# k'v of linear attention as two 64-column products per pair of heads, the pairs two at a time

## The chip, the cores and the metric

The kernel runs on one core of a Trainium2 chip. Its time is the device time of one execution in microseconds (us), as the median of several runs. A profiled execution gives the trace: for each engine (PE is TensorE's matmuls, PEld its loads of weights, DVE VectorE, ACT ScalarE, POOL GpSimd, SP the queue that issues DMAs) when each instruction began and how long it took.

## What is computed

Three layers follow each other: linear attention with a normalised output, a feed-forward layer with h cos(h) between its two matrices, and a soft mixture of experts.

```python
batch, n_heads, seq, head_dim = (8, 8, 576, 64)
kv = np.einsum('bhsd,bhse->bhde', k, v)
out = np.einsum('bhsd,bhde->bhse', q, kv)
rms = np.sqrt(np.mean(out * out, axis=-1, keepdims=True) + 1e-06)
x = (out / rms * g_norm)          # then laid out as 4608 tokens x 512
h = x @ w_in                      # 512 x 2048
g = h * np.cos(h)
x = g @ w_out                     # 2048 x 512
logits = x @ phi                  # 32 slots, softmax over tokens (d) and over slots (c)
slot_input = d.T @ x
...                               # two layers per expert on the slots
return c @ slot_out
```

The change is in the first line alone: kv, one 64 x 64 matrix for each batch and head.

## The kernel before

The 4608 tokens go through in 12 blocks of 384 (index j), and each block in 16 steps (index f) over 128 of the 2048 columns of w_in. Three blocks cover two batches (384 tokens of the one, 384 of the other, 192 of each). All is float32; h is computed in three float32r products.

In each step TensorE runs `main`, 12 matmuls of 384 columns into one of three buffers named h. The cosine chain then takes ScalarE (fr, tt), VectorE (tt), ScalarE (the sine, L401) and VectorE (gT, which frees the buffer, and the transpose tr). Between two mains stands side work that tables in PLAN place by step; a step number of 16 or more means the next block. The order on every engine is written out by these tables, and each engine follows its own queue.

The side work, by the names of its tiles: `kvps` is k'v, `ops` the attention output of 128 tokens, `xTps` their transposes, `l` the logits of four steps (four matmuls, each into 32 partitions), `lr` their sum over the four partition groups, `ldT` a transpose of the exponentials, `ab` the sum over slots, `tr` and `wps` transposes and products with w_out in the first two blocks, `eo` a product of the experts in the tail.

k'v of a batch is four calls of `kv_pair`, one for each pair of heads. A pair multiplies 128 columns of k (two heads) with 128 columns of v, over four chunks of 128 rows and one remainder of 64 (`kz`, `vr`), into 128 x 128 of PSUM. Of this only the two 64 x 64 blocks on the diagonal are wanted; two copies (L140) take them to `kvbd`, which holds the other blocks at zero.

From batch 4 on, the four pairs of a batch stand in steps 14, 17, 18 and 19 of a block. Logits stand in steps 6, 10, 14 and 18, lr in step 19. Batches 2 and 3 have a table of their own, `K`; batch 1's pairs all stand in the first step, and batch 0's ahead of it. Banks for kvps, ops, xTps, lr and others come from one pool of four, `at_bank`, in the order of the requests.

Of the kernel before, what the change touches and what calls it, by code (L numbers as in the profile page):

```python
# [40 lines left out]
    stop=None,  # L41
    start=(
# [4 lines left out]
    ),  # L47
# [17 lines left out]
    xs=(1, 1, 1),  # L65
    xT=(7, 11, 14),
    lo=(1, 0, 0),
    kv=(14, 17, 18, 19),
    rg=(11, 18),
    kvl=0,  # L70
    ql=13,
# [4 lines left out]
def tile_linear_attention__ffn_cos__soft_moe(  # L76
# [14 lines left out]
    nc = tc.nc  # L91
# [44 lines left out]
    def at_bank(name):  # L136
        return ps_a.tile([128, 512], F32, tag="at", name=name)

    def copy_on(e, out, in_):
        (nc.vector.tensor_copy if e else nc.scalar.copy)(out=out, in_=in_)  # L140


    q_t, kv_t, vr_t = {}, {}, {}
    kz = rem_p.tile([128, 2, 512], F32, tag="kr", name="kz")
# [31 lines left out]


    def kv_pair(b, pr):
        ps = at_bank("kvps")[:, 0:128]
        t = kv_t.pop((b, pr))  # L180
        for r in range(4):
            nc.tensor.matmul(out=ps, lhsT=t[:, 0, r, :], rhs=t[:, 1, r, :], start=(r == 0), stop=False)  # L182
        cc = slice(pr * 128, pr * 128 + 128)
        nc.tensor.matmul(out=ps, lhsT=kz[:, b % 2, cc], rhs=vr_t[b // 2][:, cc], start=False, stop=True)  # L184
        t = kvbd[b % 2]
        e = PLAN["ke"][b] if b < 2 else 2
        copy_on(e, t[0:64, pr, 0:64], ps[0:64, 0:64])
        copy_on(e, t[64:128, pr, 64:128], ps[64:128, 64:128])

        kv_done.add((b, pr))  # L190

# [642 lines left out]
    for b in range(1, B):  # L834
        p, i = divmod(b, 2)
        n, sl = 3 * p - 2 + i, PLAN["kv"]
        if b < 4:
            n, sl = PLAN["K"][b - 1]
        for pr in range(4):
            at2(n, sl[pr], kv_pair, b, pr)  # L840
# [96 lines left out]
    def token(t, f):  # L937
        k, *arg = t.split(".")
        if k.upper() in steps:
            out = int(k.islower())  # L940
            w = int(arg[0]) if arg else f + (PLAN["LO"] if out else PLAN["LI"])
            if w < NF and (arg or w >= (PLAN["PO"] if out else PLAN["PI"])):
                ck(k.upper(), w, out)
                steps[k.upper()](w, out)
        elif arg:
            a = int(arg[0])
            dict(kv=lambda: kv_pair(0, a), ao=lambda: att_out(0, a), xs=lambda: att_xs(0, a),
                 xT=lambda: att_xT(0, a), lo=lambda: att_lo(0, a), warm=lambda: warm(a),
                 win=lambda: load_win(a), wout=lambda: load_wout(a), lkv=lambda: load_kv(a // 4, a % 4),
                 rem=lambda: load_rem(a) if a == 0 else load_kz(0, 1), q=lambda: load_q(a))[k]()  # L950
        else:
            j = int(k[1])
            f -= L * j
            if 0 <= f < NF:
                dict(m=main, s=lambda j, f: run(side, j, f), f=fr_tt, r=round_off, p=lambda j, f: run(post, j, f),
                     b=cos_b, c=cos_c, e=lambda j, f: run(fin, j, f), l=lambda j, f: run(loads, j, f))[k[0]](j, f)
# [103 lines left out]
```

## Time and profile before

| what | value |
|---|---|
| three runs | 719.67, 717.18, 719.83 us; median 719.67 |
| profiled execution | 720.89 us |
| its span, first to last instruction | 719.0 us |
| TensorE busy | 689.0 us, 96% |
| VectorE busy | 527.1 us, 73% |
| ScalarE busy | 443.8 us, 62% |
| kvps, matmul passes of L182 and L184 | 256 and 64 |

The first three lines are times of the whole execution; the others are from the trace, where busy time is the union of an engine's instructions. A float32 matmul stands in the trace as two passes, each a load of weights (PEld) and a matmul (PE): 32 pairs of four matmuls at L182 make 256. Passes overlap, so one pass's own duration (280 ns in the mean for kvps) is longer than the distance to the next; prices are read from start to start.

### The profile page before, as it was taken

To read this page: it belongs to the slowest core of one execution; us is meant where nothing else is said; L and a number is where in the kernel's file an instruction comes from. 1 tells how busy PE (TensorE), PEld (TensorE's weight loads), DVE (VectorE), ACT (ScalarE), POOL (GpSimd) and SP (SyncE) were. 2 spreads that over 40 slices of the span, in tenths; PEclk is the share of its full clock that TensorE was granted. 3 is DMA by queue.
4 is the path that set the end of the run, shared out by engine and by line. 5 is a ranking of instruction groups with operands and counts; after the bars stand their busy time and mean duration, and the time that the engine had idled before them with its cause. 6 is when DMAs were issued, how large, how long until landed. Compare 5 with 4: busy or idle time off the path is not lost.

```text
span 719.0 us, 13016 instructions
## 1 busy us (share of the span) xinstructions
PE 689.0 (96%) x4780; PEld 574.3 (80%) x4780; DVE 527.1 (73%) x1101; ACT 443.8 (62%) x929; POOL 106.5 (15%) x104
## 2 busy tenths in 40 slices
PE   7879999999999999999999999999999999999984
PEld 7768998886998987998898879889979797864353
DVE  2998998477888878788888887888887874345144
ACT  2567997675666676575576756656757557551143
POOL 2342333100302111112012011110120210000400
PEclk9998999999999999999999999999999999999997
DMA  9953452022742674564525745735249278989997
GB/s 323 377 190 138 176 188 78 4 80 100 210 122 67 183 206 124 169 179 103 147 77 148 205 146 154 213 84 152 73 117 305 51 242 269 348 321 347 356 370 320
DMA packets 73886, 134.09 MB, mean 186 GB/s; under 512 B 8416, under 2 KB 50016, under 8 KB 73056
## 3 DMA queue, kind: packets, MB, share of 16 engines
q1 hardware_dynamic: 73824, 133.27, 58.7%
q8 instruction: 38, 0.62, 0.3%
q14 instruction: 24, 0.20, 0.1%
HBM read 91.29 MB, written 13.63 MB: 146 GB/s over the span
## 4 chain that ended last, share of the span: by engine, by line
PE 82%; DVE 9%; ACT 4%; issue 2%; DMA 1%; SPq 0%; POOL 0%; DVEq 0%; ACTq 0%
PE h L375 50%; PE ab L533 5%; PE kvps L182 4%; PE l L458 4%; PE ops L201 4%; PE xTps L233 2%; PE tr L431 2%; PE eo L689 2%; PE eh L663 2%; DVE gT L410 1%; DVE tt L396 1%; PE l L467 1%; PE fo L714 1%; PE kvps L184 1%; DVE tr L416 1%
## 5 line engine op out<-in xcount | busy, mean ns | idle before, releaser
L375 PE MATMUL h<-xt,w 128*128 128x384 f32 x2304 | 438.0, 342 | 1.6 <-DVE xt L246 1.2
L375 PEld LDWEIGHTS h<-xt,w 128*128 128x128 f32 x2304 | 397.2, 189 | 29.1 <-DVE gT L410 8.9
L401 ACT ACTIVATE fr<-tt 128x384 f32<-128x384 f32 x192 | 100.4, 524 | 136.5 <-DVE tt L396 136.0
L410 DVE TENSOR_TENSOR gT<-fr,h 128x384 f32<-128x384 f32 x186 | 102.8, 553 | 58.6 <-ACT fr L401 58.4
L213 POOL TENSOR_TENSOR ri<-ss,mhalf 128x8 f32<-128x8 f32 x36 | 65.5, 1825 | 430.8 <-DVE ss L211 430.8
L396 DVE SCALAR_TENSOR_TENSOR tt<-tt,fr 128x384 f32<-128x384 f32 x192 | 106.5, 559 | 28.9 <-ACT tt L391 27.5
L391 ACT ACTIVATE tt<-fr 128x384 f32<-128x384 f32 x192 | 100.9, 525 | 6.1
L389 ACT ACTIVATE fr<-h 128x384 f32<-128x384 f32 x192 | 92.7, 483 | 18.2 <-PE h L375 18.0
L416 DVE STREAM_TRANSPOSE tr<-gT 128x384 f32<-128x384 f32 x144 | 83.3, 579 | 5.1 <-DVE gT L410 0.2
L237 ACT ACTIVATE xt<-xTps,gn 128x512 fp32r<-128x512 f32 x36 | 24.6, 686 | 27.8 <-PE xTps L233 27.4
L182 PEld LDWEIGHTS kvps<-kv 128*128 128x128 f32 x256 | 31.8, 191 | 9.9 <-issue 6.4
L201 PE MATMUL ops<-kvA,q 128*64 128x128 f32 (+1 forms) x384 | 38.2, 278 | 1.3 <-ACT g L140 1.3
L201 PEld LDWEIGHTS ops<-kvA,q 128*64 128x64 f32 (+1 forms) x384 | 33.9, 164 | 5.2 <-issue 2.8
L182 PE MATMUL kvps<-kv 128*128 128x128 f32 x256 | 35.2, 280 | 1.8 <-DMA kv<-in_kv 1.7
L246 DVE SCALAR_TENSOR_TENSOR xt<-xTps,gn,xt 128x512 fp32r<-128x512 f32 x36 | 26.4, 738 | 12.8 <-ACT xt L237 12.5
L313 POOL TENSOR_TENSOR w<-st_m,w 128x512 fp32r<-128x512 f32 x16 | 26.7, 1670 | 54.3 <-ACT w L308 41.1
L533 PE MATMUL ab<-g,d 128*32 128x512 f32 x288 | 33.5, 596 | 0.3 <-DVE d L522 0.3
L458 PE MATMUL l<-gT,wp 128*32 128x384 f32 x312 | 33.3, 498 | 0.0
L140 ACT COPY g<-tr 128x384 f32<-128x384 f32 (+1 forms) x64 | 23.4, 393 | 7.7 <-PE tr L431 7.4
L210 DVE TENSOR_REDUCE ss<-sq 128x8 f32<-128x512 f32 x33 | 22.2, 672 | 5.0 <-ACT sq L208 4.8
L208 ACT ACTIVATE sq<-ops 128x512 f32<-128x512 f32 x33 | 19.6, 593 | 9.1 <-PE ops L201 9.1
L222 DVE TENSOR_TENSOR xs<-ops,ri 128x512 f32<-128x512 f32 x33 | 22.3, 682 | 2.4 <-POOL ri L213 2.4
(133 smaller groups left out, 631.3 us busy)
## 6 DMA issues: line engine op xcount, KB each, us to landing
g<-tr SPq DMA_DIRECT2D x288, 96.0 KB
kv<-in_kv SPq DMA_DIRECT2D x32, 512.0 KB
ew<-in_w SPq DMA_DIRECT2D x26, 512.0 KB
ew<-in_w SPq DMA_DIRECT2D x43, 256.0 KB
out<-ot SPq DMA_DIRECT2D x12, 768.0 KB
q<-in_qT SPq DMA_DIRECT2D x11, 768.0 KB
rw<-in_w_in SPq DMA_DIRECT2D x16, 512.0 KB
st_b<-in_w_outT SPq DMA_DIRECT2D x16, 512.0 KB
```

The lines of the kernel that those rows point to most:

```text
L182: nc.tensor.matmul(out=ps, lhsT=t[:, 0, r, :], rhs=t[:, 1, r, :], start=(r == 0), stop=False)
L201: nc.tensor.matmul(out=ps[p0:p0 + n, pr * 128:(pr + 1) * 128], lhsT=q_t[j][:, pr, c0:c0 + n], rhs=kvbd[b % 2][:, pr, :], start=True, stop= ...
L213: nc.gpsimd.tensor_tensor(out=ri[:, :, 0], in0=ss, in1=mhalf, op=ALU.pow)
L375: nc.tensor.matmul(out=ps, lhsT=w[:, a, kk, :], rhs=x[:, b, kk, :], start=(n == 0), stop=(n == 3 * KD - 1))
L389: nc.scalar.activation(out=fr, in_=ps, func=AF.Copy, bias=0.25, scale=INV_2PI)
L391: nc.scalar.activation(out=tt, in_=fr, func=AF.Copy, bias=ROUND_M)
L396: nc.vector.scalar_tensor_tensor(out=tt, in0=tt, scalar=-ROUND_M, in1=fr, op0=ALU.add, op1=ALU.subtract)
L401: nc.scalar.activation(out=fr, in_=tt, func=AF.Sin, scale=-TWO_PI_DOWN)
L410: nc.vector.tensor_tensor(out=g, in0=fr, in1=h_t.pop((j, f)), op=ALU.mult)
L416: nc.vector.transpose(out=tr_t[j, h][:, :, o, :], in_=g.rearrange("p (b t) -> p b t", t=32))
L458: nc.tensor.matmul(out=l_t[j][32 * o:32 * o + 32, :], lhsT=wp[:, f, :], rhs=gT_t.pop((j, f)), start=(c == 0), stop=(c == (2 if j == NB - 1 ...
L533: nc.tensor.matmul(out=ps[32 * c:32 * c + 32, :], lhsT=d[:, t, :], rhs=gs[c // 2][t][:, (c % 2) * 512:(c % 2) * 512 + 512], start=(t == 0) ...
```

## The change

`kv_pair` no longer forms the full 128 x 128 product. For each chunk it issues two matmuls, one per head: 64 columns of k and 64 of v into partitions 0 to 63 or 64 to 127 of the bank, both in columns 0 to 63. The second copy reads its block at the new place. In the table, the second pair of a batch moves from step 17 to step 14 and the fourth from step 19 to step 18, from batch 4 on.

```diff
-    kv=(14, 17, 18, 19),
+    kv=(14, 14, 18, 18),
...
     def kv_pair(b, pr):
-        ps = at_bank("kvps")[:, 0:128]
+        ps = at_bank("kvps")[:, 0:64]
         t = kv_t.pop((b, pr))
+        hh = [slice(0, 64), slice(64, 128)]
         for r in range(4):
-            nc.tensor.matmul(out=ps, lhsT=t[:, 0, r, :], rhs=t[:, 1, r, :], start=(r == 0), stop=False)
-        cc = slice(pr * 128, pr * 128 + 128)
-        nc.tensor.matmul(out=ps, lhsT=kz[:, b % 2, cc], rhs=vr_t[b // 2][:, cc], start=False, stop=True)
+            for h in hh:
+                nc.tensor.matmul(out=ps[h], lhsT=t[:, 0, r, h], rhs=t[:, 1, r, h], start=(r == 0), stop=False)
+        for h in hh:
+            cc = slice(pr * 128 + h.start, pr * 128 + h.stop)
+            nc.tensor.matmul(out=ps[h], lhsT=kz[:, b % 2, cc], rhs=vr_t[b // 2][:, cc], start=False, stop=True)
         t = kvbd[b % 2]
         e = PLAN["ke"][b] if b < 2 else 2
         copy_on(e, t[0:64, pr, 0:64], ps[0:64, 0:64])
-        copy_on(e, t[64:128, pr, 64:128], ps[64:128, 64:128])
+        copy_on(e, t[64:128, pr, 64:128], ps[64:128, 0:64])
```

On TensorE, in a block that holds the pairs of batch 4, from the logits of step 14 to the main of step 20, before:

```order
L458 MATMUL l<-gT,wp 32x384 x4
L182 MATMUL kvps<-kv 128x128 x4
L184 MATMUL kvps<-vr,kz 128x128
L233 MATMUL xTps<-ident,xs 128x128 x4
L375 MATMUL h<-xt,w 128x384 x36
L182 MATMUL kvps<-kv 128x128 x4
L184 MATMUL kvps<-vr,kz 128x128
L375 MATMUL h<-xt,w 128x384 x12
L458 MATMUL l<-gT,wp 32x384 x4
L182 MATMUL kvps<-kv 128x128 x4
L184 MATMUL kvps<-vr,kz 128x128
L375 MATMUL h<-xt,w 128x384 x12
```

and of the change, the same place (its lines stand three further down):

```order
L461 MATMUL l<-gT,wp 32x384 x4
L184 MATMUL kvps<-kv 64x64 x8
L187 MATMUL kvps<-vr,kz 64x64 x2
L184 MATMUL kvps<-kv 64x64 x8
L187 MATMUL kvps<-vr,kz 64x64 x2
L236 MATMUL xTps<-ident,xs 128x128 x4
L378 MATMUL h<-xt,w 128x384 x48
L461 MATMUL l<-gT,wp 32x384 x4
L184 MATMUL kvps<-kv 64x64 x8
L187 MATMUL kvps<-vr,kz 64x64 x2
L184 MATMUL kvps<-kv 64x64 x8
L187 MATMUL kvps<-vr,kz 64x64 x2
```

Each group of logits now has two pairs behind it, and between the two groups four mains (48 matmuls) follow each other without other work; lr in step 19 has no pair behind it any more.

On VectorE, the same block in step 14 and the steps behind it, before:

```order
L416 STREAM_TRANSPOSE tr<-gT 128x12x32
L140 COPY kvA<-kvps 64x64 x2
L246 SCALAR_TENSOR_TENSOR xt<-xTps,gn,xt 128x4x128
L396 SCALAR_TENSOR_TENSOR tt<-tt,fr 128x384
L292 TENSOR_SCALAR st_m<-st_m 128x256
```

and of the change:

```order
L419 STREAM_TRANSPOSE tr<-gT 128x12x32
L140 COPY kvA<-kvps 64x64 x4
L249 SCALAR_TENSOR_TENSOR xt<-xTps,gn,xt 128x4x128
L399 SCALAR_TENSOR_TENSOR tt<-tt,fr 128x384
L295 TENSOR_SCALAR st_m<-st_m 128x256
```

The four copies of both pairs now stand ahead of the tt of step 14; in step 18 it is the same, and steps 17 and 19 have none.

On TensorE around the last three pairs of batch 2, before (the change alters only the kvps rows here, to 64x64 x8 and x2):

```order
L467 MATMUL l<-gT,wp 32x384 x2
L182 MATMUL kvps<-kv 128x128 x4
L184 MATMUL kvps<-vr,kz 128x128
L375 MATMUL h<-xt,w 128x384 x24
L483 MATMUL lr<-ls,rep 128x384
L520 MATMUL ldT<-ident,ld 128x64 x3
L182 MATMUL kvps<-kv 128x128 x4
L184 MATMUL kvps<-vr,kz 128x128
L375 MATMUL h<-xt,w 128x384 x24
L533 MATMUL ab<-g,d 32x512 x12
```

Here the pairs keep their places: one directly behind two logits, one behind lr and ldT, and the last one (further down) behind logits and ldT. ldT reads only 64 rows of weights.

## Rows read from the trace of the kernel before

**Rows 1.** Page: busy time of the engines, and the last chain by engine.

```profile
PE 689.0 (96%) x4780; PEld 574.3 (80%) x4780; DVE 527.1 (73%) x1101; ACT 443.8 (62%) x929; POOL 106.5 (15%) x104
...
PE 82%; DVE 9%; ACT 4%; issue 2%; DMA 1%; SPq 0%; POOL 0%; DVEq 0%; ACTq 0%
```

**Rows 2.** Windows: stretch, length, busy us per engine, granted clock, DMA share, GB/s.

```profile
324.00:374.00 50.00, 50.00 (x334) 43.82 (x333) 40.98 (x93) 31.48 (x63) 5.58 (x3) 1.00 0.43 111
```

**Rows 3.** Timeline of PE, 345 to 360 us: start, length, line, tile, passes.

```profile
345.02 6.50 PE L375 MATMUL h<-xt,w 128*128 128x384 f32 x36
351.35 1.05 PE L182 MATMUL kvps<-kv 128*128 128x128 f32 x8
...
352.38 2.36 PE L375 MATMUL h<-xt,w 128*128 128x384 f32 x12
354.68 0.85 PE L458 MATMUL l<-gT,wp 128*32 128x384 f32 x8
355.46 1.16 PE L182 MATMUL kvps<-kv 128*128 128x128 f32 x8
...
356.60 2.35 PE L375 MATMUL h<-xt,w 128*128 128x384 f32 x12
358.79 0.81 PE L483 MATMUL lr<-ls,rep 128*128 128x384 f32 x2
359.43 1.05 PE L182 MATMUL kvps<-kv 128*128 128x128 f32 x8
```

**Rows 4.** Timeline of PE, 201 us: two pairs of batch 3.

```profile
201.09 1.05 PE L182 MATMUL kvps<-kv 128*128 128x128 f32 x8
...
202.20 1.06 PE L182 MATMUL kvps<-kv 128*128 128x128 f32 x8
```

**Rows 5.** Groups by line and form: busy us and mean ns, idle before.

```profile
L182 PEld LDWEIGHTS kvps<-kv 128*128 128x128 f32 x256 | 31.8, 191 | 9.9 <-issue 6.4 <-DMA kv<-in_kv 1.9 <-PE kvps L184 0.2
...
L140 DVE COPY kvA<-kvps 64x64 f32<-64x64 f32 x56 | 12.1, 216 | 2.5 <-PE kvps L184 1.6
...
L201 PEld LDWEIGHTS ops<-kvA,q 128*64 128x64 f32 x192 | 10.2, 136 | 2.6 <-issue 2.6
```

**Rows 6.** Timeline of PE, 261 us: ops in its 64-wide form.

```profile
261.80 1.09 PE L201 MATMUL ops<-kvA,q 128*64 128x128 f32 x16
262.82 4.88 PE L375 MATMUL h<-xt,w 128*128 128x384 f32 x24
```

**Rows 7.** Timeline of PEld, 261 us: loads of the same, and a wait of h.

```profile
261.79 0.85 PEld L201 LDWEIGHTS ops<-kvA,q 128*64 128x64 f32 x16 [0.25 <-issue]
...
265.34 2.04 PEld L375 LDWEIGHTS h<-xt,w 128*128 128x128 f32 x12 [0.47 <-DVE gT L410]
```

**Rows 8.** Timeline of PE, 62 us: eight passes into four strips.

```profile
62.42 0.43 PE L321 MATMUL wps<-st_a,phi_sb 128*32 128x128 f32 x8
62.66 0.81 PE L467 MATMUL l<-gT,wp 128*32 128x384 f32 x4
```

**Rows 9.** Windows, eo (L689) alone: length, busy PE and PEld, clock, DMA.

```profile
681.00:684.20 3.20, 3.20 (x64) 1.95 (x60) 1.00 1.10 348
```

**Rows 10.** Timeline of PE, 29 to 34 us: the four pairs of batch 1.

```profile
29.25 1.16 PE L182 MATMUL kvps<-kv 128*128 128x128 f32 x8
...
32.92 1.13 PE L182 MATMUL kvps<-kv 128*128 128x128 f32 x8
...
34.03 2.33 PE L375 MATMUL h<-xt,w 128*128 128x384 f32 x12
```

**Rows 11.** Windows of the start-up, columns as in rows 2.

```profile
18.00:20.00 2.00, 0.97 (x7) 0.77 (x5) 2.00 (x4) 0.69 (x1) 2.00 (x2) 0.64 1.02 406
...
30.00:32.00 2.00, 2.00 (x20) 2.00 (x19) 1.97 (x4) 1.40 (x2) 0.00 (x0) 1.00 1.11 393
```

**Rows 12.** Timeline of ACT, 254 us: the sines of two plain steps.

```profile
254.39 0.53 ACT L401 ACTIVATE fr<-tt 128x384 f32<-128x384 f32 x1 [0.74 <-DVE tt L396]
...
256.60 0.52 ACT L401 ACTIVATE fr<-tt 128x384 f32<-128x384 f32 x1 [0.74 <-DVE tt L396]
```

## Prediction

> **What bounds the kernel now.** I read the page first. TensorE is busy for 96% of the span, and the chain that ended last runs through it for 82% [rows 1]. An average over stages says little of one stage, so I asked for the stretches next: between 324 and 374 us, which hold the products k'v of two batches, TensorE is busy in all 50.00 us at the full granted clock, VectorE in 40.98 and ScalarE in 31.48 [rows 2]. From about 60 us to 600 us it looks like that. There every microsecond taken off TensorE's queue is a microsecond of the span, as long as the cosine chain on ScalarE and VectorE keeps up. The timeline of TensorE then gives the price of each piece, from the start of one piece to the start of the next [rows 3]. The start-up (to 60 us) is another matter: there DMA and VectorE end the waits.
>
> **What a pair costs now.** Each float32 matmul stands in the trace as two passes, each with its own load of weights; a pair of heads is five matmuls, so ten passes. Two pairs back to back start at 201.09 and 202.20: 1.11 us, 111 ns per pass of 128 columns [rows 4].
>
> **What a pair costs after.** It has twenty passes of 64 columns into 64 partitions, alternately the lower and the upper half of the array's columns. Three things set their price.
> First, the length of a pass follows its columns: two passes of 384 columns take 0.64 us (358.79 to 359.43), 0.32 each or 107 ns per 128 [rows 3]. For 64 columns that makes 54 to 56 ns; I take 57. The load shrinks alike: 191 ns for 128 columns of weights, 136 for 64, so 55 less [rows 5].
> Second, whether both halves run side by side. The nearest row is ops in its 64-wide form: 16 passes of 128 columns in 1.02 us [rows 6]. One after the other they would need 16 x 0.111 = 1.78; two at a time 8 x 0.111 = 0.89, and 0.13 is left for a change of form. Their loads start (0.85 - 0.136) / 15 = 48 ns apart [rows 7], less than half of 111. So they do.
> Third, whether passes can be issued so fast. Side by side means one pass every 28 ns. The nearest short burst has it: eight passes of wps between 62.42 and 62.66, 30 ns each [rows 8]. Over a longer stretch the fastest that the trace shows is eo, 64 passes in 3.20 us, 50 ns each, which its 256 columns explain by themselves [rows 9].
> So a pair takes 10 x 0.057 = 0.57 us, 0.54 less. The bounds are 0.53 (nothing but the columns) and, if twenty passes came one behind the other, 1.14.
>
> **What changes of form cost.** The logits use 32 columns of the array at a time, the kv passes now 64, all else 128. An h run of 12 passes takes 2.19 before lr and 2.30 before logits (0.11 to go in); the logits take 0.78 where four at a time they need 2 x 0.32 = 0.64 (0.14 to come out) [rows 3]. A pair among 128-wide work now pays both ways; I take 0.30, a little above 0.11 + 0.14. A pair directly behind logits only adds one stop on the way back: 0.15.
>
> **The sum.**
> - Batches 4 to 7: two groups each, logits and then two pairs. Before, four pairs cost 4 x 1.11; after, a group saves 2 x 0.54 - 0.15 = 0.93. Eight groups: 7.4 us.
> - Batch 2: one pair between 128-wide pieces saves 0.54 - 0.30 = 0.24; three stand behind logits or ldT, which have left the 128 form already: 3 x 0.39. Together 1.4.
> - Batch 3: two single pairs 2 x 0.24, one double 1.08 - 0.30 = 0.78. Together 1.3.
> - Batch 1: four pairs in one step, from 29.25 to 34.03, the last held up by its load until 32.92 [rows 10]. What the first three save is waited off there; the last ends after 0.57 + 0.15 and not 1.11: 0.4 us.
> - Batch 0: up to 2 us of TensorE at 7.7 us, but DMA is full to beyond 32 us [rows 11] and the wait at 32.92 comes after it. I count nothing.
> - Copies: as many as before, 216 ns each [rows 5]. Two move from step 17 to 14, two from 19 to 18. They delay tt of their step by 0.43 us; a group now gives TensorE 1.14 + 0.15 us more work than a step without pairs, which covers it; without that cover, 8 x 0.43 = 3.4 us would be at stake. A bank is reused after four requests; the one that the second pair of a group takes was last read several steps earlier. Loads wait for a pair to free their buffer, and pairs 1 and 3 free it sooner.
> - Behind batch 7 nothing differs: the loads there are released by TensorE's progress and move with it.
>
> Sum: 7.4 + 1.4 + 1.3 + 0.4 = 10.5 us. The profiled execution took 720.89 us (span 719.0 and 1.9 around it), which gives 710.4; the median shown, 719.67, lies 1.2 lower and gives 709.2. I say **709.8 us**.
>
> **Rivals.**
> *B, the cosine chain catches up.* Between the two groups of a block four steps of h now stand without any other work (before, a pair broke them up). A plain step costs TensorE 6.33 / 3 = 2.11 us (36 passes from 345.02 to 351.35 [rows 3]), but ScalarE's sines stand 2.21 apart in such steps (254.39, 256.60), since fr, tt, tt and the sine wait for each other across two engines [rows 12]. Four steps lose 4 x 0.10 = 0.4 us. For it: in a block without pairs TensorE's loads waited 0.47 for gT at 265.34 [rows 7]. Against it: that block has less work than any block after the change, three buffers of h soak up a step's delay, and the wait came behind the exponentials alone. If both waits came in all four blocks, 4 x (0.4 + 0.47) = 3.5 us would be given back: 713.3 us.
> *C, passes this short cannot come every 28 ns.* The place is the kv passes alone. The trace shows 30 ns only for a burst of eight; a group has forty. The change breaks even where 24 pairs save no more than their changes of form cost, 8 x 0.15 + 0.30 + 0.45 + 0.90 = 2.85 us: 24 x (1.11 - 20 p) = 2.85 gives p = 50 ns per pass. Above it the kernel is slower. At 57 (the halves not side by side): 24 x 0.03 = 0.7 lost and 2.85, 724.4 us against 720.89. At 68 (each half waits for its whole load of 136 ns [rows 5]): 24 x 0.25 + 2.85 = 8.9, 729.8 us. For it: no row with 64 columns in the moving operand and two halves at once. Against it: ops, whose loads and halves did just that at 128 columns.
> A rule of the Trainium skill speaks for C: "TensorE: Matmul & The Clock Gate", section "Wait — 56ns, not 53.3ns?", gives some 62 ns per matmul to the sequencer where hardware decode is off. By it a pair would take 1.24 us and the sum would be 727 us; the trace's 30 and 50 ns per pass speak against it here.
> *That nothing changes* is excluded: the order of instructions shows the 64-wide matmuls and the groups.
> One more bound: in 18 to 20 us the granted clock is 0.64 of full, behind a spell in which TensorE waited [rows 11]. TensorE now waits about 1.8 us before the last pair of batch 1; a spell of 1.2 GHz there could cost up to 2 us, and one of those that stand could go.
>
> **How the numbers follow.** The sum as it stands: 76 in 100, by itself 706 to 712.5 (no cost for the extra changes and something of batch 0 at the low end; passes at 33 ns or a slow clock at the high end). B: 14. C: 10. To leave out no more than 2 in 10 the range reaches over B's price: 705.5 to 716.5. A measurement of this kernel can tell some 0.5%, 3.6 us, from no change. The first case and nearly all of B are faster: 0.88. C near its break-even: 0.03 the same. The rest of C: 0.09 slower.
>
> **What would show it.** In the profile after: kvps with 64x64 forms, 640 passes and not 320; a group of forty passes about 1.15 to 1.2 us long, starts of weight loads under 30 ns apart on average; 1.3 us from the end of the logits to the next piece. If forty passes take more than 2 us, the second or third step (side by side, issue) is wrong. If they take 1.2 but the blocks of batches 4 to 7 shrink by less than 1.8 us each, look for h waiting on gT: B. If the extra change shows more than 0.3 us, the third term is.

## The result, and the profile after

The changed kernel takes 709.74 us in the median (708.50 to 711.72), the kernel before 719.09 beside it on the same chip: a ratio of 0.9869, with a 95% interval from 0.9848 to 0.9891. That is 9.4 us less; the prediction said 709.8. The profiled execution took 710.92 us, with a span of 709.1.

From the page of after: the engines, the chain that ended last, and the two groups of the products (busy us, mean ns, idle before).

```profile
PE 677.0 (95%) x5100; PEld 559.0 (79%) x5100; DVE 525.2 (74%) x1101; ACT 441.8 (62%) x929; POOL 106.2 (15%) x104
...
PE 69%; DVE 16%; ACT 7%; DMA 3%; issue 2%; SPq 1%; DVEq 0%; ACTq 0%
...
L184 PEld LDWEIGHTS kvps<-kv 128*64 128x64 f32 x512 | 17.6, 137 | 12.0 <-issue 7.0
...
L184 PE MATMUL kvps<-kv 128*64 128x64 f32 x512 | 20.7, 226 | 3.9 <-DMA kv<-in_kv 2.2
```

TensorE's share of the chain falls from 82% [rows 1] to 69%, and VectorE and ScalarE together now hold 23% where they held 13%: the first sign that TensorE has lost some of its lead. There are 512 passes of L184 and 128 of L187, the 640 foretold, and a load takes 137 ns (136 was taken from [rows 5]).

Windows of after, 324 to 374 us, columns as in [rows 2]:

```profile
324.00:374.00 50.00, 49.72 (x382) 43.08 (x379) 41.97 (x95) 31.41 (x64) 5.94 (x4) 1.00 0.43 113
```

TensorE was busy in all 50.00 us here; now 0.28 us are idle. The timeline of TensorE says where, for one batch:

```profile
336.94 0.85 PE L461 MATMUL l<-gT,wp 128*32 128x384 f32 x8
337.73 0.69 PE L184 MATMUL kvps<-kv 128*64 128x64 f32 x16
338.24 0.29 PE L187 MATMUL kvps<-vr,kz 128*64 128x64 f32 x4
338.36 0.64 PE L184 MATMUL kvps<-kv 128*64 128x64 f32 x16
338.82 0.29 PE L187 MATMUL kvps<-vr,kz 128*64 128x64 f32 x4
339.04 0.66 PE L236 MATMUL xTps<-ident,xs 128*128 128x128 f32 x4
339.45 8.58 PE L378 MATMUL h<-xt,w 128*128 128x384 f32 x48
347.96 0.85 PE L461 MATMUL l<-gT,wp 128*32 128x384 f32 x8
...
352.27 0.81 PE L486 MATMUL lr<-ls,rep 128*128 128x384 f32 x2
352.62 2.54 PE L378 MATMUL h<-xt,w 128*128 128x384 f32 x12
354.99 1.05 PE L204 MATMUL ops<-kvA,q 128*128 128x128 f32 x8
355.80 2.33 PE L378 MATMUL h<-xt,w 128*128 128x384 f32 x12
358.42 2.37 PE L378 MATMUL h<-xt,w 128*128 128x384 f32 x12 [0.28 <-DVE gT L413]
```

The group behind the logits of step 14 runs from 337.73 to 339.04: 1.31 us for forty passes and the step back to 128 columns, as foretold. The passes come in twos, one for each half of the columns: the trace records starts at 337.833 and 337.840, then at 337.892 and 337.898, so two every 58 ns, or 29 ns a pass in the mean. The h behind ops is that of step 21, and the next, that of step 22, waits for gT of step 19. It starts 2.62 us after the one ahead of it; in the kernel before that step took 2.17. Between 240 and 540 us the view of waits has one row for TensorE's matmuls (PE) on gT, and none in the kernel before:

```profile
PE h L378 <- DVE gT L413: 1.1, 4, 0.3
```

Four waits, one for each of the batches 4 to 7. The loads of weights (PEld), which run ahead of the matmuls, show the same wait at its full length. Their rows, first before, then after:

```profile
PEld h L375 <- DVE gT L410: 6.4, 10, 0.8
PEld h L378 <- DVE gT L413: 8.7, 14, 0.8
```

Four waits more, and 2.3 us more in all, 0.57 a batch. The ten that both kernels have lie at other steps, and at step 22 of the blocks without pairs: there h waited already before the change [rows 7]. This is rival B, at one place of the two and on top of a gain that is otherwise there.

The pairs that stand alone, in batch 3 (timeline of TensorE, after):

```profile
188.77 0.69 PE L184 MATMUL kvps<-kv 128*64 128x64 f32 x16
...
189.50 4.44 PE L378 MATMUL h<-xt,w 128*128 128x384 f32 x24
...
197.76 0.69 PE L184 MATMUL kvps<-kv 128*64 128x64 f32 x16
...
199.08 6.51 PE L378 MATMUL h<-xt,w 128*128 128x384 f32 x36
```

One pair adds 0.94 us between two h runs (measured from the last pass before it to the fourth behind it, less four passes) and two add 1.52: 0.58 for a pair and 0.36 for both changes of form. Behind logits forty passes add 1.295, so the extra change is 1.295 - 2 x 0.58 = 0.14.

**A yardstick.** The program repeats itself block by block, 16 steps of h each, so that a block's length (first pass of h to first pass of the next block's h) can be read far more finely than a median. Three blocks hold two of the batches 4 to 7. They take 146.13 us before and 143.38 after, and the next three the same within 0.05. The three blocks that hold batches 2 and 3 take 157.28 and 154.77. Behind the six blocks with batches 4 to 7 the span still has 177.1 us in both. This gives 2.5 + 2 x 2.75 = 8.0 us of the 9.4. What else the two profiles differ by (1.8 us) lies in the first 92 us, and is taken up with the fifth experiment. The interval of the ratio, 7.8 to 10.9 us, holds the 8.0 as well as the 9.4.

### The profile page after: what moved, and what is told of

It is laid out like the page before. It is cut to its first block, busy times and chain, and to the rows that moved or that the text cites. A ratio compares the mean times of both kernels' runs of the same rounds, so it can differ in the third digit from the quotient of the medians.

```text
span 709.1 us, 13637 instructions
## 1 busy us (share of the span) xinstructions
PE 677.0 (95%) x5100; PEld 559.0 (79%) x5100; DVE 525.2 (74%) x1101; ACT 441.8 (62%) x929; POOL 106.2 (15%) x104
## 4 chain that ended last, share of the span: by engine, by line
PE 69%; DVE 16%; ACT 7%; DMA 3%; issue 2%; SPq 1%; DVEq 0%; ACTq 0%
PE h L378 42%; PE ab L536 5%; PE l L461 3%; DVE gT L413 3%; PE ops L204 3%; DVE tr L419 3%; DVE tt L399 2%; PE xTps L236 2%; ACT fr L404 2%; PE tr L434 2%; PE eo L692 2%; PE eh L666 2%; DMA kv<-in_kv 2%; ACT L404 1%; PE fo L717 1%
## 5 line engine op out<-in xcount | busy, mean ns | idle before, releaser
L184 PEld LDWEIGHTS kvps<-kv 128*64 128x64 f32 x512 | 17.6, 137 | 12.0 <-issue 7.0
L184 PE MATMUL kvps<-kv 128*64 128x64 f32 x512 | 20.7, 226 | 3.9 <-DMA kv<-in_kv 2.2
```

What stands on the lines that cost most here:

```text
L184: nc.tensor.matmul(out=ps[h], lhsT=t[:, 0, r, h], rhs=t[:, 1, r, h], start=(r == 0), stop=False)
```

## The experiments

Each ran beside the kernel before. "Three blocks" are the first three with batches 4 to 7, in the profiled execution.

| kernel | median us | ratio to before, 95% interval | three blocks us |
|---|---|---|---|
| before | 718.9 to 720.0 | 1 | 146.13 |
| after | 709.74 | 0.9869 [0.9848, 0.9891] | 143.38 |
| split alone | 710.69 | 0.9888 [0.9859, 0.9918] | 143.62 |
| steps alone | 719.28 | 1.0006 [0.9989, 1.0022] | 146.46 |
| head by head | 716.43 | 0.9970 [0.9956, 0.9984] | 145.18 |
| a step ahead of logits | 712.02 | 0.9899 [0.9872, 0.9927] | 143.55 |
| start at 128 columns | 710.07 | 0.9883 [0.9862, 0.9903] | 143.39 |
| second group at 17 | 710.50 | 0.9880 [0.9857, 0.9903] | 143.18 |
| all four at 17 | 710.82 | 0.9888 [0.9868, 0.9907] | 142.85 |
| copies behind tt | 714.11 | 0.9930 [0.9910, 0.9949] | 145.50 |
| weights two steps earlier | 713.59 | 0.9929 [0.9906, 0.9952] | 144.27 |
| exponentials a step later | 715.01 | 0.9940 [0.9920, 0.9959] | 144.66 |
| the same weights, batch 3 grouped | 714.30 | 0.9929 [0.9905, 0.9954] | 144.13 |
| two copies a group | 708.86 | 0.9860 [0.9841, 0.9879] | 142.69 |

**1 and 2. The two halves of the change apart.** First the 64-column products at the old steps, then the 128-column product at the new ones:

```diff
-    kv=(14, 14, 18, 18),
+    kv=(14, 17, 18, 19),
```

> The 64-column pairs, with the pairs left in steps 14, 17, 18 and 19. My theory (a pair costs 0.57 us of TensorE and 0.30 to 0.35 for two changes of form, or 0.15 to 0.18 behind logits): batches 4 to 7 save 8 x 0.18 and 8 x 0.37 = 4.4 us, the batches before them keep what they save, 4.3 us, and the wait for gT in step 22 (0.5 us in each of four blocks of the changed kernel) goes, since step 19 has a pair again. In all 8.7 us under before, some 710.4. Rival: the grouping makes the gain in batches 4 to 7, so that they save 1 us or less here: 714 to 716. Spare sign: a lone pair between h runs takes 0.9 us, not 1.1.

```diff
-        ps = at_bank("kvps")[:, 0:64]
+        ps = at_bank("kvps")[:, 0:128]
...
-            for h in hh:
-                nc.tensor.matmul(out=ps[h], lhsT=t[:, 0, r, h], rhs=t[:, 1, r, h], start=(r == 0), stop=False)
+            nc.tensor.matmul(out=ps, lhsT=t[:, 0, r, :], rhs=t[:, 1, r, :], start=(r == 0), stop=False)
```

> The full 128-column pairs of before, with the table of the change (14, 14, 18, 18). My theory: TensorE has the same work, so the time is that of before, 719.1, within 1 us; two pairs of 1.11 us in step 18 give the chain behind gT more cover than in the changed kernel, so its wait in step 22 is 0 to 0.2 us. Rival (grouping makes the gain): 714 to 716. Second rival (moving copies and pairs hurts the cosine chain): 721.

The split alone brings 8.2 of the 9.4 us; the steps alone nothing. In the blocks the split is worth 2.51 us, the grouping on top of it 0.24. It should have added more, since it saves two trips out of the 128 form and back a batch; what it gains is waited off at step 22. By the medians the two kernels with the split are not told apart; that reading rests on the blocks.

**3. One head after the other.** The same 64-column passes, all ten of one head ahead of the other's:

```diff
-        for r in range(4):
-            for h in hh:
+        for h in hh:
+            for r in range(4):
```

> The changed kernel with the loops of a pair turned round: all five chunks of the first head, then those of the second, so that passes of the same half of the array follow each other. My theory (the two halves run side by side only when neighbouring passes lie in different halves): a pair takes 20 x 0.057 = 1.14 us and not 0.57, a group of two 2.28; 24 pairs lose 13.7 us, less some 2 us of waits that go: 720 to 722. Rival (short columns alone make the gain, or TensorE finds the overlap by itself): 710, a group of 1.15 to 1.3 us.

The order matters, as expected, but a lone pair adds 1.35 us and not 1.14 + 0.36 = 1.50. The passes of one half stand 58 ns apart in either order; in the alternating one each has one of the other half 6 to 7 ns behind it. Head by head the two heads still overlap by a little: see the last section. A group behind logits takes 1.94 us from its first pass to the next piece, against 1.31 in after and 2 x 1.14 for two pairs in the kernel before, so that this kernel stands between the two, and between the two times expected.

**4. Away from the logits, one step earlier.**

```diff
-    kv=(14, 14, 18, 18),
+    kv=(13, 13, 17, 17),
```

> The changed kernel with the groups one step earlier, in steps 13 and 17, where no logits stand ahead of them. My theory: each of eight groups pays two changes of form and not one, 0.17 us more: 1.4 us, 711. Rival A (the place behind logits is worth nothing): 709.7 and groups that cost the same 1.3 us. Rival B (the wait in step 22 hangs on cover in step 18): the waits grow by up to 1 us in each of four blocks, 714.

Forty passes alone add 1.516 us and behind logits 1.295: the place behind the logits is worth 0.22 a group. Yet the three blocks, with four groups, are only 0.17 longer and not 4 x 0.22 = 0.88, because most of the wait at step 22 is gone. The matmuls have no row of it any more; the loads still wait there, 0.27 us (timeline of PEld):

```profile
359.05 2.05 PEld L378 LDWEIGHTS h<-xt,w 128*128 128x128 f32 x12 [0.27 <-DVE gT L413]
```

In after it is 0.60. That showed that the wait could be made shorter by other means, and asked what makes it.

**5. The start-up.** Pairs of batches 0 and 1 stay one 128-column product:

```diff
     def kv_pair(b, pr):
+        if b < 2:
+            return kv_pair_full(b, pr)
```

> The changed kernel, but the pairs of batches 0 and 1 stay one 128-column product each (batches 2 to 7 as changed). It prices the start-up, for which the prediction counted 0.4 us (batch 1) and nothing (batch 0). In the profile after, the first block of the changed kernel is 1.8 us shorter than before, but part of that is a shorter stretch at the half clock, and these stretches differ from run to run. The medians less the later blocks leave 0.7 to 1.3 us. Theory: the halves are worth about 1 us at the start, so this kernel takes 710.7 us. Rival 1: nothing, since DMA and VectorE's copies set the pace there: 709.7. Rival 2: all 1.8 us: 711.5.

It takes 710.07 us, 0.3 more than after, with intervals that overlap nearly whole. That lies nearer to rival 1, but the medians alone do not tell my 1 us from nothing. What differs from run to run there is the granted clock. Windows of 51 to 61 us, before, after, and this kernel:

```profile
51.00:61.00 10.00, 8.17 (x41) 7.51 (x42) 8.76 (x14) 5.18 (x11) 1.58 (x2) 0.66 0.67 238
```

```profile
51.00:61.00 10.00, 8.96 (x60) 8.28 (x62) 8.04 (x13) 5.98 (x13) 1.48 (x1) 0.83 0.56 193
```

```profile
51.00:61.00 10.00, 8.74 (x65) 7.20 (x66) 8.81 (x16) 7.01 (x15) 2.11 (x2) 1.00 0.67 236
```

The mean clock is 0.66, 0.83 and 1.00, and the first block ends at 92.36, 90.52 and 89.44 us. In three profiles with 1.00 here it ends at 89.05 (split alone), 89.08 (steps alone, 128 columns at the start) and 89.44 (this one, 128 columns): among these the halves are worth 0 to 0.4 us at the start. A fourth (head by head, 64 columns) ends at 88.50; it has no stretch at half the clock around 20 us, as the other three have.

**6 and 7. The groups elsewhere.**

```diff
-    kv=(14, 14, 18, 18),
+    kv=(14, 14, 17, 17),
```

> The changed kernel with the second group one step earlier: pairs at steps 14, 14, 17, 17 and not 14, 14, 18, 18. Step 17 has no logits in front, so the second group stands alone among 128-wide work: one more change of form, 0.2 us a block, four blocks: +0.9. In the changed kernel h of step 22 waits for gT of step 19 (0.28 us in each of four blocks, about 0.5 lost with what follows). Theory: the wait comes from the four copies that VectorE makes in step 18 ahead of that step's tt; in step 17 they meet less work on VectorE, the wait goes, 4 x 0.5 = 2.0 back: 709.7 - 2.0 + 0.9 = 708.6 us. Rival: the wait comes from the steps without other work for TensorE behind the last group; it stays (those steps are one more then), and 709.7 + 0.9 = 710.6.

```diff
-    kv=(14, 14, 18, 18),
+    kv=(17, 17, 17, 17),
```

> All four pairs of a batch in step 17: one group of eighty passes alone among 128-wide work. Eighty passes at 29 ns are 2.3 us, and one change of form in and out 0.35: 2.67 a block against 0.96 + 0.93 saved of 4.46, that is 2.57 now. So TensorE's work is 0.1 a block more. Theory: eight copies stand behind the group on VectorE (8 x 0.22 = 1.75 us), ahead of a tt; but TensorE has 2.67 us more work there, which covers them, and the wait of 0.5 a block goes: 709.7 + 0.4 - 2.0 = 708.1. Rival: eight copies hold up the cosine chain more than four do, the wait grows by 0.9 a block: 709.7 + 0.4 + 3.5 = 713.6.

In both the matmuls have none of the four waits of 0.3 us that after has (the one row left, 0.15 us, lies in a block without pairs); the loads still wait 0.26 to 0.27 us there, as in the fourth experiment. So most of the wait went, and not all of it, as the theory said. The three blocks are shorter by 0.20 and 0.53. The medians are 0.8 and 1.1 longer than after's, with intervals over one another; both profiled executions have a mean clock of 0.984 against 0.988. By the medians neither theory is told from the other; by the blocks the theory's direction holds, at a third of its size in the first and two thirds in the second.

**8. The same copies, behind tt.** From batch 4 on, the four copies of a group are issued behind the step's tt on VectorE and not ahead of it; TensorE's order is untouched.

```diff
+            if b >= 4:
+                late2(n, sl[pr], kv_copy, b, pr)
```

> The changed kernel, but from batch 4 on the copies of a group out of its bank are issued behind the step's tt on VectorE and not ahead of it; TensorE's order is untouched. It tells apart what makes h of step 22 wait for gT. Theory: the four copies (0.93 us) ahead of tt in step 18 delay the sines of steps 18 and 19 and so gT; without them the wait vanishes, 4 x 0.5 = 2.0 us come back, and 707.7 us is measured. Rival: the wait comes since four steps behind the group have nothing but h for TensorE (2.11 a step against 2.21 for the chain on ScalarE and VectorE); VectorE's copies are then the same work at another place, the wait stays, and 709.7 is measured.

Both fell: it is 4.4 us slower than after. Timelines of VectorE, first of after, then of this kernel:

```profile
350.23 0.52 DVE L480 COPY ls<-l 128x384 f32<-128x384 f32 x1
350.68 0.93 DVE L140 COPY kvA<-kvps 64x64 f32<-64x64 f32 x4
351.64 0.56 DVE L399 SCALAR_TENSOR_TENSOR tt<-tt,fr 128x384 f32<-128x384 f32 x1
...
357.81 0.56 DVE L413 TENSOR_TENSOR gT<-fr,h 128x384 f32<-128x384 f32 x1 [0.92 <-ACT fr L404]
```

```profile
354.52 0.54 DVE L409 SCALAR_TENSOR_TENSOR tt<-tt,fr 128x384 f32<-128x384 f32 x1
354.98 0.94 DVE L140 COPY kvA<-kvps 64x64 f32<-64x64 f32 x4
...
361.64 0.55 DVE L423 TENSOR_TENSOR gT<-fr,h 128x384 f32<-128x384 f32 x1 [0.92 <-ACT fr L414]
```

From tt of step 18 to gT of step 19 it is 6.17 us in after and 7.12 here. The copies have left the link ahead of tt and lengthened the next one: gT of step 18 and the row maximum mb stand behind them in VectorE's queue. And h of step 17 now waits too, behind the copies of the first group (timeline of TensorE):

```profile
342.25 4.42 PE L388 MATMUL h<-xt,w 128*128 128x384 f32 x24
346.99 4.55 PE L388 MATMUL h<-xt,w 128*128 128x384 f32 x24 [0.32 <-DVE gT L423]
...
362.25 0.96 PE L388 MATMUL h<-xt,w 128*128 128x384 f32 x4 [0.60 <-DVE gT L423]
```

**9 and 10. Is it the sum of VectorE's work?** The preparation of the output weights two steps earlier (part of those weights is then computed from other data, here and in experiment 11, so that only time is read), and the exponentials one step later:

```diff
-    nt=(1, (12, 16, 20, 24), (1, 2), (2, 1), (3, 1), 4),
+    nt=(1, (10, 14, 18, 22), (1, 2), (2, 1), (3, 1), 4),
```

> The changed kernel, with the preparation of the output weights (st_m on VectorE and ScalarE, four times a block) two steps earlier; pairs and copies stay at steps 14 and 18. In the changed kernel VectorE has no idle time from 349.1 to 355.6 us, from the copies of the second group to the row maximum of the logits, and st_m takes 0.7 us of it. The last run showed that copies behind tt make the wait longer. Theory now: it is the sum of VectorE's work between the end of that group and the row maximum that makes h of step 22 wait; with 0.7 us of other work taken out of it the wait of 0.28 goes, and 4 x 0.5 = 2.0 us come back: 707.7 us; blocks of batches 4 to 7 sum to 141.3 to 142.3 us for three and not 143.4. Rival: the wait is set by the four copies' own place ahead of tt in step 18 (tt of step 18 is just as late), and stays: 709.7 and 143.4.

```diff
-    le=18,
-    la=19,
-    lx=(3, 1),
+    le=19,
+    la=20,
+    lx=(4, 1),
```

> The changed kernel, with the row maximum and the exponentials of the logits one step later (copy of the logits at step 19 and not 18, row maximum and exponentials at 20 and not 19), so that the copies of the second group and the exponentials no longer meet in one stretch of VectorE. Theory (sum of VectorE's work in one stretch): the wait at step 22 goes, 707.7 us. Rival: the exponentials' own chain (two table loads of 1.28 us on ScalarE) sets the wait and it moves to step 23 with no less: 709.7 us.

The sum of VectorE's work is not the cause. With the weights away VectorE has time to spare behind the copies (0.59 idle), and h of step 22 waits longer. Timelines of VectorE and of TensorE:

```profile
351.92 0.93 DVE L140 COPY kvA<-kvps 64x64 f32<-64x64 f32 x4
352.88 0.56 DVE L399 SCALAR_TENSOR_TENSOR tt<-tt,fr 128x384 f32<-128x384 f32 x1
354.02 0.55 DVE L413 TENSOR_TENSOR gT<-fr,h 128x384 f32<-128x384 f32 x1 [0.59 <-ACT fr L404]
...
358.93 0.55 DVE L413 TENSOR_TENSOR gT<-fr,h 128x384 f32<-128x384 f32 x1 [1.25 <-ACT fr L404]
```

```profile
340.49 8.58 PE L378 MATMUL h<-xt,w 128*128 128x384 f32 x48
...
359.54 2.38 PE L378 MATMUL h<-xt,w 128*128 128x384 f32 x12 [0.37 <-DVE gT L413]
```

With the exponentials later the wait moves to step 23, as the rival had it, and grows: at 715.01 us the kernel is 5 us slower than the rival said. In blocks without pairs the matmuls, which do not wait there in after, now wait 0.64 to 0.66 us as well (timeline of TensorE, exponentials later):

```profile
363.82 2.38 PE L378 MATMUL h<-xt,w 128*128 128x384 f32 x12 [0.84 <-DVE gT L413]
```

**11. Both, with batch 3 grouped.** The weights as in the ninth, and batch 3's pairs at 14, 14, 18, 18.

```diff
-    K=((0, (0, 0, 0, 0)), (2, (-2, 3, 1, 6)), (2, (15, 12, 19, 15))),
+    K=((0, (0, 0, 0, 0)), (2, (-2, 3, 1, 6)), (2, (14, 14, 18, 18))),
```

> The weights two steps earlier as above, and batch 3's four pairs as two groups behind logits too (steps 14 and 18). Batch 3's pairs cost 0.94 + 1.52 + 0.93 = 3.4 us as they stand in the changed kernel, two groups behind logits 2 x 1.295 = 2.6. Theory: 707.7 - 0.8 = 706.9 us. Rival (wait unchanged, batch 3 adds a wait of 0.5): 709.7 - 0.8 + 0.5 = 709.4.

Batch 3's block becomes 1.0 us shorter (54.78 to 53.77), and the next one 1.4 longer than with the earlier weights alone (46.96 to 48.38). One pair more stands in the next block now, yet it has less work for TensorE there, by some 0.4 us from step to step. The gain was waited off: the four copies of the first group stand ahead of the two xt on VectorE, and h of the next block's first step waits 0.81 us for xt; and the wait of step 22 is there, 0.51 us. At 714.30 us neither number that was expected came.

**12. A shorter chain.** The third theory: what counts is the length of the cosine chain from one group to the end of the exponentials, whatever it consists of. A group's two pairs lie side by side in one bank, and two copies take them out:

```diff
+    def kv_two(b, pr):
+        ps = at_bank("kvps")[:, 0:128].rearrange("p (a c) -> p a c", c=64)
...
+        for h in hh:
+            copy_on(2, t[h, pr:pr + 2, h], ps[h])
```

> The changed kernel, but the two pairs of a group go into one bank, side by side, and are copied out by two copies of 64 x 2 x 64 and not four of 64 x 64; TensorE's order is untouched. Reading so far: from h of step 15 to h of step 22 TensorE's own work takes 18.46 us (358.42 less the 0.51 by which step 22 starts late, less 339.45), and the cosine chain from step to step takes 18.97, of which four copies ahead of tt in step 18 are 0.93; in the runs with other places for the copies or with less other work on VectorE the chain stayed within 0.15 of that. Theory: the chain itself is the bound there, and only work taken off it helps. Copies of 128 elements a row cost some 0.25 each (the copy of 128x96 out of a bank takes 0.22 to 0.24), two of them 0.5: the chain becomes 18.5, the wait goes but for 0.1, and 4 x 0.4 = 1.6 us come back: 708.1 us, blocks of batches 4 to 7 142.5 us for three and not 143.4. Rival: a copy of 64 x 2 x 64 takes as long as two (0.43), or the wait has another cause: 709.7 us and 143.4.

The theory held, at a little less than its size. Of this kernel the group of such copies (lines by form), its place on VectorE, and TensorE at step 15 and at steps 21 and 22:

```profile
L140 DVE COPY kvA<-kvps 64x128 f32<-64x128 f32 x16 | 4.6, 285 | 0.8 <-PE kvps L188 0.6
```

```profile
348.75 0.57 DVE L140 COPY kvA<-kvps 64x128 f32<-64x128 f32 x2
349.35 0.56 DVE L415 SCALAR_TENSOR_TENSOR tt<-tt,fr 128x384 f32<-128x384 f32 x1
...
355.54 0.55 DVE L429 TENSOR_TENSOR gT<-fr,h 128x384 f32<-128x384 f32 x1 [0.92 <-ACT fr L420]
```

```profile
337.53 8.58 PE L394 MATMUL h<-xt,w 128*128 128x384 f32 x48
...
353.88 4.65 PE L394 MATMUL h<-xt,w 128*128 128x384 f32 x24
```

Two copies take 0.57 us and not 0.93; h of steps 21 and 22 is one run again, and the matmuls have no row of the wait any more. The row of the loads has the fourteen waits of after, with 1.3 us less:

```profile
PEld h L394 <- DVE gT L429: 7.4, 14, 0.8
```

The kernel also takes one bank for a group and not two, but no load of kvps waits for VectorE in this stretch, here or in after. The blocks are 0.69 shorter, 1.4 us over the four batches. The median, 708.86, is 0.9 below after's, and 10.5 below that of the kernel before beside it; the two intervals overlap, so that this step is shown by the trace and not by the medians.

## Why the prediction was right, and where it was off

**Which limit, where.** Right: in the stretch of batches 4 to 7 TensorE's queue set the span, and the split of the product is what shortened it (experiments 1 and 2).

**A pair, 0.57 us.** Right: 0.58, 29 ns a pass in the mean, over forty passes in a row. Experiment 3 confirms the mechanism: without the alternation a lone pair costs 1.35 us. Rival C did not come. The rule of the Trainium skill that spoke for it ("TensorE: Matmul & The Clock Gate", section "Wait — 56ns, not 53.3ns?", some 62 ns a matmul where hardware decode is off) does not bind as the prediction read it, by the pass: the trace has two passes every 58 ns, 6 to 7 ns from one to the other. Counted by the program's matmuls, of two passes each, one comes every 58 ns, too close to 62 for this case to settle it, and whether hardware decode is on, no run shows.

**Changes of form.** 0.14 behind logits (0.15 predicted), 0.36 alone (0.30 predicted). Experiment 4 gives 0.22 for the place behind logits.

**Batches 4 to 7, 7.4 us.** Here the sum was off, in the step that put the copies at no cost ("a group now gives TensorE 1.14 + 0.15 us more work than a step without pairs, which covers it"). From the start of one h to the next, a batch saves 1.03 at step 17, gives 0.22 more at steps 14 and 18, and saves 1.13 at 19 and 20: 1.95 in all, or 7.8 for four, a little more than was said. But steps 21 and 22 give back 0.57, so that 1.375 is left: 5.5 us. The prediction compared a group with a step, and missed that the cover is a balance over many steps. From the start of h of step 15 to gT of step 19 the chain takes 363.98 - 345.02 = 18.96 us before ([rows 3], and on VectorE):

```profile
363.98 0.56 DVE L410 TENSOR_TENSOR gT<-fr,h 128x384 f32<-128x384 f32 x1 [0.92 <-ACT fr L401]
```

So h of step 22 could have started 0.6 behind that, at 19.6; TensorE came there only after 20.6. After, TensorE's own work comes down by 2.1 to 18.5, and the chain does not let h of step 22 start before 18.97:

| kernel | h 15 | gT 19 | difference | h 22 starts after |
|---|---|---|---|---|
| after | 339.45 | 357.81 | 18.36 | 18.97 |
| copies behind tt | 342.25 | 361.64 | 19.39 | 20.00 |
| weights earlier | 340.49 | 358.93 | 18.44 | 19.05 |
| two copies | 337.53 | 355.54 | 18.01 | 18.62 |

In all four h of step 22 stands 0.61 behind the start of gT: the chain sets it, also where only the loads are seen to wait. In the kernel before and in the split alone, whose loads do not wait there in blocks with pairs, it stands 1.65 and 1.4 behind. The expectation of experiment 12 said that the chain had stayed within 0.15 us in the other runs; with the copies behind tt it was 1.03 longer. What lies on that chain counts (copies ahead of tt, or of gT and the row maximum), and what lies on VectorE beside it does not.

**Rival B** came at step 22 alone. Its price was put at 0.87 a block and measured 0.57, of which two copies a group bring back 0.35. The remaining 0.22 is the same wait, shorter: step 21 takes 2.27 with two copies, 2.61 in after and 2.17 before; step 22 takes 3.40 to 3.43 where its h stands 0.61 behind gT, and 3.29 before. What else of the chain could be shortened was not tried. The four plain steps for which rival B also allowed do not wait, but its reason is at work in them: there gT follows gT by 2.20 us (342.55, 344.75, 346.95, 349.14 in after) and h follows h by 2.08, so that the chain falls back by 0.12 us a step. The sign named for B in the prediction came too: the blocks shrink by 1.375 us a batch, less than 1.8.

**Batches 2 and 3**: 2.7 predicted, 2.5 measured. **Batches 0 and 1**: 0.4 predicted, 0 to 0.4 measured, and for a reason that was misread. From the first pair of batch 1 to the h behind the last it is 4.78 us before and 4.36 after, as was said; how much of it reaches the end of the first block stays open. The last pair of batch 1 was said to be "held up by its load". In after it waits for VectorE, which has yet to copy the earlier pairs out of their banks:

```profile
32.08 0.69 PE L184 MATMUL kvps<-kv 128*64 128x64 f32 x16 [1.66 <-DVE kvA L140]
```

**The sum.** 2.5 + 5.5 + 0 to 0.4 make 8.0 to 8.4, against 10.5 predicted; the medians beside each other differ by 9.4. The remaining 1 us is no more than what one profile differs from the next in the first 92 us (the first block ends at 88.5 to 92.4 us, with the granted clock), and it lies inside the interval of the medians. So the prediction had the mechanism and the larger part of the size, but that 709.74 us came so close to 709.8 was luck: 2 us that the chain took back were missed; about 1 us of the medians' difference is not shown to be the change's; and the kernel before, from whose 719.67 us the prediction counted, came out 0.6 us lower beside the change.

## What to carry to other kernels

Two products that fill half the array's columns each can run side by side if their passes alternate in program order: look at the starts of the passes in the trace, not only at their number. When work is taken off the bounding engine, compare whole stretches, from the last common start to the next thing waited for: no more can be gained there than down to the length of the second chain, and what lies on it (here four small copies) is the next thing to shorten. Where a measurement's spread is as large as the question, the length of a repeated block in the trace answers it.

## What had not been expected of the hardware

TensorE's passes do not start strictly in the order of the program. In the head-by-head kernel the program has eight passes of L184 and two of L186 for one head, then the same for the other. The timeline of TensorE shows ten of L184 first, and then the lines by turns:

```profile
188.33 0.73 PE L184 MATMUL kvps<-kv 128*64 128x64 f32 x10
188.84 0.22 PE L186 MATMUL kvps<-vr,kz 128*64 128x64 f32 x1
188.90 0.22 PE L184 MATMUL kvps<-kv 128*64 128x64 f32 x1
188.90 0.22 PE L186 MATMUL kvps<-vr,kz 128*64 128x64 f32 x1
188.95 0.46 PE L184 MATMUL kvps<-kv 128*64 128x64 f32 x5
```

The second head's first pass is recorded at 188.730, while three passes of the first head start at 188.783, 188.841 and 188.899. So the other half of the columns began some three passes early, and 17 x 0.058 + 0.36 = 1.35 us is what the pair costs, and not 20 x 0.058 + 0.36 = 1.52. The Trainium skill ("PSUM — Partial Sum Buffer", section "Engine vs sequencer instructions") says that matmuls start and complete in program order; the starts recorded here show otherwise for two halves of the columns. Whether more than three passes can be taken ahead was not tried.
